# Threshold attention and a SwiGLU block on one core: the first batch's softmax scalings go to GpSimd

## The chip, the cores and the metric

The kernel runs on one core of one Trainium2 chip. A core has a matrix engine (TensorE, "PE" in the profile, with its weight loads as "PEld"), a vector engine (VectorE, "DVE"), a scalar engine (ScalarE, "ACT"), a general engine (GpSimd, "POOL") and a queue engine (SyncE, "SP") that issues most transfers. Each engine executes its own list of instructions in the order in which the program wrote them, and waits in front of an instruction whose operands are not ready. Results of TensorE land in a small accumulation memory of eight banks (PSUM); everything else lives in the on-chip memory (SBUF) with 128 partitions.

The metric is the device time of one execution in microseconds (us). The kernel before took 1361.29 us, the median of three runs (1361.02 to 1361.42).

## The reference

The inputs are q, k and v of 8 batches, 8 heads, 576 positions and 64 values each, a threshold tau, and the three weight matrices of a feed-forward block (512 to 1536 twice, 1536 to 512). Everything is float32.

```python
scores = (q @ k.T) / sqrt(64)
scores = where(scores >= max(scores) - tau, scores, -1e9)
attn = exp(scores - max(scores));  attn = attn / (sum(attn) + 1e-9)
x = (attn @ v)   # (8, 8, 576, 64), laid out as 4608 tokens of 512 values
g = x @ w_gate
out = (g * sigmoid(g) * (x @ w_val)) @ w_out
```

The attention of a batch needs all keys at once; the feed-forward block needs all eight heads of a token.

## The kernel before

The work goes through in two forms. **The first batch** (batch 0) is written out by hand. Its eight heads are four pairs; a pair's 576 queries are cut into four tiles of 128 rows (t = 0 to 3) and a tile of 64 rows (t = 4), in which both heads share the partitions. First the two early tiles (t = 0 and 1) of all four pairs are done, while keys, queries, values and weights are still arriving; then the tiles t = 2, 3 and 4 of all four pairs. The weights arrive in a raw form of two 32-bit words per number and are rebuilt beside the attention: ACT splits a piece (L330, L331), POOL clamps it (L323), DVE shifts it (L350) and joins its sign (L356), POOL adds its lower word (L366). Which of these steps comes after which point of which tile is written in the table `STEPS`, and in the second part in the loop itself.

**The other seven batches** form 84 slots. A planner (`Plan`) keeps a clock per engine, and every job carries an estimated duration. It emits the jobs of DVE, ACT, POOL and SP in the order of the estimated starts; the order on PE is that of the program. The estimates therefore set only the order, not the time.

One tile of the first batch passes through `scores` in five steps, and the loop over the tiles puts the steps of neighbouring tiles between each other:

1. The score products (L463) go into two PSUM tiles, one for each head, each of two banks. There are just these two tiles, so a product has to wait until the mask of the tile before has read the same head's scores. Then DVE finds each row's maximum (L480).
2. ACT forms the threshold (L483) and the exponentials (L484).
3. DVE masks them and sums the rows (L487), and forms the reciprocal `ri` of the sum (L489, L490). For t >= 2, head 0 is then scaled by `ri` on ACT (L497) and head 1 on POOL (L495).
4. For t < 2 the probabilities stay unscaled. In the next tile's turn ACT writes two diagonal matrices, `ident` times `ri` (L503).
5. After the next tile's score products and after the products with v of the tile before (`attend_tile`, L564 and L566), `flip_steps` turns the probabilities on PE: for t >= 2 by a transpose against the identity (L531, L539), for t < 2 by an ordinary product with the diagonal matrix (L533, L537), which scales in passing. ACT copies the result out of PSUM (L540, L547).

In the second part of the first batch the loop also puts products of the first feed-forward unit between the tiles (`fill`, L580, with L595, L596 on ACT, L604 on DVE and L611 on POOL). In tile t = 3 the first half of the turn of tile t = 2 stands ahead of the exponentials.

In POOL's own list a step of `scores` stands ahead of the clamp and the addition that the loop emits after it, and behind those that the loop emitted before it. Other POOL scalings are those of the queries: L403 in the first batch, L1912 in the slots, and L1847, which scales some of head 1's probabilities in the slots (the tables `POOLED` and `FIRST_POOLED` say how many).

All POOL scalings have one operation, such as

```python
nc.gpsimd.tensor_scalar(out=ps[x], in0=ps[x], scalar1=ri[:, x:x + 1], scalar2=None, op0=ALU.mult)
```

while the clamp, also on POOL, has two operations with constants (`min`, then `max`).

Of the kernel before, what the change touches and what calls it, by code (L numbers as in the profile page):

```python
# [14 lines left out]
ALU = mybir.AluOpType  # L15
# [129 lines left out]
def kernel(  # L145
# [107 lines left out]
    dbufs = deque(room(2 * P).rearrange("p (h q) -> p h q", h=2) for _ in range(2))  # L253
# [130 lines left out]
    def load_qk(i):  # L384
# [17 lines left out]
        def scale(x):  # L402
            nc.gpsimd.tensor_scalar(out=x, in0=x, scalar1=scl, scalar2=None, op0=ALU.mult)  # L403
# [50 lines left out]
    def scores(seg, t):  # L454
        qT, kT = seg["qT"], seg["kT"]
        q0 = t * P - seg["q0"]
        if t < NT:
            pss = [ps_s.tile([P, 2, 512], F32, name="sc") for _ in range(2)]
            for h, hs in enumerate(heads):
                cut_ = D if turned(t) and h == 1 else 0  # L460
                for n, lo, to in [(0, 0, D), (0, D, SH), (1, 0, SH)] if cut_ else [(0, 0, SH), (1, 0, SH)]:
                    at_ = (n * SH + lo - cut_) % S
                    nc.tensor.matmul(pss[h][:, n, lo:to], qT[hs, q0:q0 + P], kT[hs, at_:at_ + to - lo],  # L463
                                     start=True, stop=True)
# [26 lines left out]
        units = [ident] * m  # L491
        if t >= TA:
            for x in range(m):
                if x % 2:
                    nc.gpsimd.tensor_scalar(out=ps[x], in0=ps[x], scalar1=ri[:, x:x + 1], scalar2=None, op0=ALU.mult)  # L495
# [8 lines left out]
        unflipped.append((seg, t, both, [(p.rearrange("p n s -> p (n s)"), unit) for p, unit in zip(ps, units)]))  # L504
# [9 lines left out]
    def flip_steps():  # L514
# [8 lines left out]
        for h, (p, unit) in enumerate(ps):  # L523
# [3 lines left out]
            for kt in range(KT):  # L527
                at_ = kt * P + (D if turned(t) and h == 1 else 0)
                ks, to = slice(at_, at_ + P), slice(kt * P, (kt + 1) * P)
                if unit is ident:  # L530
                    nc.tensor.transpose(tp[:, to], p[:, ks], unit)  # L531
                else:
                    nc.tensor.matmul(tp[:, to], p[:, ks], unit, start=True, stop=True)  # L533
            if t < NT:
                if h == 1 and not turned(t):
                    for hs, (p_, unit_) in zip(heads, ps):
# [1598 lines left out]
```

## Time and profile before

| What | us |
|---|---|
| Median of three runs | 1361.29 |
| Profiled execution: first to last instruction (its own time is listed only as this span) | 1360.6 |
| PE busy | 1345.4 |
| DVE busy | 1067.0 |
| ACT busy | 880.6 |
| POOL busy | 714.9 |
| First tile's score products start (L463) | 7.83 |
| First score products of the second part of the first batch (t = 2) | 47.92 |
| First slot's score products start (L1776) | 128.88 |
| Granted clock of TensorE | 1.000 |

A line of a group in the profile reads: line of the kernel, engine, operation, output tile from input tiles, shapes, count, then busy time in us and the mean of one in ns, then the idle time of the engine just before and what ended it. A line of the timeline reads: start, length, engine, line, operation, tiles, shape, count, and in brackets the idle time before it and what ended that. A float32 product appears as two records, since TensorE goes over it twice; a transpose against the identity appears as one. The length of a merged line runs to the modelled end of its last record, so lines of one engine overlap a little; how long a group occupies PE is the distance to the start of the next group. A line of the waits reads: who waited for whom, the sum in us, the number of times and the longest.

### The profile page before, as it was taken

Reading aid. Unit: us, or ns where it says so; the run is one execution under the profiler, and the core shown is the slowest. Engines: PE = TensorE matmul, PEld = TensorE weight load, DVE = VectorE, ACT = ScalarE, POOL = GpSimd, SP = SyncE. Lnnn points to the kernel's source line nnn. Section 1 sums busy time; section 2 is a strip of 40 time slices with the busy share of each in tenths; the row PEclk is TensorE's granted clock in tenths of the full one; section 3 lists DMA queues with packets and bytes.
Section 4 is the critical chain, followed back from the end, with each engine's and each line's share of the span. In section 5 each row is a group of like instructions: output and inputs, shape, how many; then the busy total and the mean of one; then the engine's idle time right before and its main releaser. Section 6 shows DMA issues by size and latency. Waiting matters only on the chain.

```text
span 1360.6 us, 39192 instructions
## 1 busy us (share of the span) xinstructions
PE 1345.4 (99%) x15590; PEld 1112.3 (82%) x15590; DVE 1067.0 (78%) x2815; ACT 880.6 (65%) x2280; POOL 714.9 (53%) x662
## 2 busy tenths in 40 slices
PE   9999999999999999999999999999999999999998
PEld 7777777787788788877887788877887788999998
DVE  7788898878887777787778877877778776787786
ACT  6888777777756767676766776776767674330330
POOL 3788497654565679434963387427943592000000
PEclk9999999999999999999999999999999999999999
DMA  8753323555425531654154514553155404424411
GB/s 184 200 181 98 77 60 110 163 157 144 138 52 160 147 93 36 194 145 114 37 172 129 156 30 131 140 148 87 52 178 145 114 27 141 159 78 147 158 60 32
DMA packets 208294, 162.32 MB, mean 119 GB/s; under 512 B 166128, under 2 KB 180464, under 8 KB 202736
## 3 DMA queue, kind: packets, MB, share of 16 engines
q1 hardware_dynamic: 204192, 158.90, 41.5%
q8 instruction: 124, 2.03, 0.6%
q10 hardware_dynamic: 3920, 0.92, 0.3%
q14 instruction: 58, 0.48, 0.1%
HBM read 138.28 MB, written 21.50 MB: 117 GB/s over the span
## 4 chain that ended last, share of the span: by engine, by line
PE 92%; DVE 3%; DMA 2%; POOL 1%; ACT 1%; issue 1%; SPq 1%; ACTq 0%; DVEq 0%; POOLq 0%
PE pb L1047 18%; PE pa L1047 12%; PE px L1529 12%; PE sc L1776 10%; PE xa L1873 9%; PE pe L1047 9%; PE po L1326 5%; PE py L1538 5%; PE pv L1251 2%; PE pg L1251 2%; PE sc L1208 2%; PE pe L1208 1%; PE sc L463 1%; PE sc L1529 1%; POOL pall L495 1%
## 5 line engine op out<-in xcount | busy, mean ns | idle before, releaser
L1824 DVE SCALAR_TENSOR_TENSOR pall<-sc,th,pall 128x288 f32<-128x288 f32 x504 | 243.8, 513 | 60.5 <-ACT pall L1822 43.8
L1047 PE MATMUL pb<-xall,big 128*128 128x256 f32 x1152 | 273.3, 380 | 0.0
L1822 ACT ACTIVATE pall<-sc,nm 128x288 f32<-128x288 f32 x504 | 232.0, 496 | 38.8 <-DVE pall L1824 38.7
L1047 PEld LDWEIGHTS pb<-xall,big 128*128 128x128 f32 x1152 | 216.5, 190 | 30.7 <-issue 2.5
L1852 DVE STREAM_TRANSPOSE pall<-pall 128x576 f32<-128x576 f32 x252 | 188.0, 762 | 32.0 <-ACT pall L1850 18.4
L1850 ACT ACTIVATE pall<-pall,ri 128x288 f32<-128x288 f32 x418 | 191.7, 527 | 24.5 <-DVE ri L1838 23.8
L1047 PE MATMUL pa<-xall,big 128*128 128x256 f32 x768 | 183.6, 382 | 0.0
L900 POOL TENSOR_TENSOR hall<-hall,tmp 128x512 f32<-128x512 f32 x80 | 102.3, 1279 | 138.7 <-DVE hall L1100 122.1
L1797 DVE TENSOR_REDUCE mx<-sc 128x2 f32<-128x576 f32 x168 | 125.3, 746 | 52.4 <-PE sc L1776 51.9
L1047 PEld LDWEIGHTS pa<-xall,big 128*128 128x128 f32 x768 | 142.9, 190 | 22.4 <-issue 4.3
L1776 PE MATMUL sc<-kT,qT 64*32 64x288 f32 (+1 forms) x5376 | 146.1, 345 | 2.6 <-issue 2.1
L1776 PEld LDWEIGHTS sc<-kT,qT 64*32 64x32 f32 x5376 | 94.9, 106 | 56.7 <-issue 21.4
L1047 PE MATMUL pe<-xall,big 128*128 128x256 f32 x576 | 137.2, 381 | 0.6 <-issue 0.6
L1873 PE MATMUL xa<-pall,vall 64*32 64x288 f32 x4032 | 128.9, 404 | 0.0
L1847 POOL TENSOR_SCALAR pall<-pall,ri 128x288 f32<-128x288 f32 x86 | 85.2, 1003 | 81.1 <-DVE ri L1838 80.4
L1047 PEld LDWEIGHTS pe<-xall,big 128*128 128x128 f32 x576 | 108.5, 190 | 17.4 <-issue 3.0
L1873 PEld LDWEIGHTS xa<-pall,vall 64*32 64x32 f32 x4032 | 73.9, 107 | 47.2 <-issue 5.6
L1832 ACT COPY sums<-sums 32x6 f32<-32x6 f32 x336 | 66.6, 198 | 29.6 <-DVE pall L1824 24.5
L900 POOL TENSOR_TENSOR tmp<-tmp 128x512 f32<-128x512 f32 x36 | 45.9, 1276 | 59.3 <-ACT tmp L1122 59.3
L1099 ACT ACTIVATE vall<-tmp 128x512 f32<-128x512 f32 x96 | 60.0, 628 | 25.6 <-DVE tmp L1112 10.3
L1538 PE MATMUL py<-wo,hall 128*128 128x256 f32 x336 | 74.8, 379 | 0.0
L1799 DVE TENSOR_REDUCE mx<-sc 128x1 f32<-128x288 f32 x168 | 74.7, 445 | 0.0
(258 smaller groups left out, 2473.9 us busy)
## 6 DMA issues: line engine op xcount, KB each, us to landing
big<-sums_hbm SPq DMA_DIRECT2D x42, 1024.0 KB, 5.3
big<-sums_hbm SPq DMA_DIRECT2D x48, 768.0 KB, 4.7
vall<-in_v_dram SPq DMA_DIRECT2D x112, 144.0 KB, 3.1
out_dram<-big SPq DMA_DIRECT2D x32, 256.0 KB, 3.3
qT<-in_q_dram SPq DMA_DIRECT2D x112, 72.0 KB, 4.8
kT<-in_k_dram SPq DMA_DIRECT2D x112, 72.0 KB, 3.1
wo<-in_moe_w_gate_dram SPq DMA_DIRECT2D x16, 384.0 KB, 3.8
wo<-in_moe_w_val_dram SPq DMA_DIRECT2D x16, 384.0 KB, 4.4
```

Source lines behind the costliest of these rows:

```text
L900: return lambda: nc.gpsimd.tensor_tensor(out=out, in0=a, in1=b, op=op)
L1047: nc.tensor.matmul(ps[:, i], w[:, k_, i * P:(i + 1) * P], x[:, k_, :], start=first and i == k_ == 0, stop=True, skip_group_check=True)
L1529: nc.tensor.matmul(ps, a[:, f, :], ws[n][:, f, :], start=bank_ not in begun, stop=True, skip_group_check=True)
L1538: nc.tensor.matmul(ps(), a[:, f, i * P:(i + 1) * P], operands[o][:, f, :], start=first and f == 0, stop=True, skip_group_check=True)
L1776: nc.tensor.matmul(pss[h][(slice(g * G, (g + 1) * G), *part)], qT[hs, col:col + G], kT[hs, c * SH + keys[0]:c * SH + keys[1]], start=True, ...
L1797: rs.append(job("DVE", 0.72, lambda n=n, tile_=tile_: nc.vector.tensor_reduce(out=mx[:, n:n + 2, 0], in_=tile_[:, :, 0:SH], axis=AX.X, op= ...
L1822: ej = job("ACT", 0.42, lambda x=x, n=n: nc.scalar.activation(ps[x], scs[x], AF.Exp, bias=nm[:, n:n + 1]), ej, masks.get((h, u - 1)), rank=0)
L1824: masks[x] = job("DVE", 0.45, lambda x=x, n=n: nc.vector.scalar_tensor_tensor(out=ps[x], in0=scs[x], scalar=th[:, n:n + 1], in1=ps[x], op0 ...
L1847: scaled.append(job("POOL", 1.02, lambda x=x, n=n: nc.gpsimd.tensor_scalar(out=x, in0=x, scalar1=ri[:, n:n + 1], scalar2=None, op0=ALU.mul ...
L1850: scaled.append(job("ACT", 0.46, lambda x=x, n=n: nc.scalar.activation(x, x, AF.Copy, scale=ri[:, n:n + 1]), rj, rank=rank))
L1852: seg["turned"].append(job("DVE", 0.72, lambda both=both: nc.vector.transpose(out=both, in_=both), *scaled, rank=rank))
L1873: nc.tensor.matmul(holds[a].ap()[x * G:(x + 1) * G, 0:SH].rearrange("d (i q) -> d i q", q=G), vr[rs, h, j, ds], p[rs, h, :, j, :], start=( ...
```

## The change

Every scaling on POOL gets a second operation, a multiplication by the constant 1.0. In the first batch every probability is scaled on POOL right after `ri`: for t < 2 both heads, which were not scaled there before, and for t >= 2 both heads, of which ACT scaled head 0 before. For t = 4 the one tile moves from ACT to POOL. The diagonal matrices are gone, with their buffers, and all full 128-column turns are transposes against the identity; the products that turn the last 64 keys (L537) stay ordinary products, now with the identity. The score products of a tile come in the order head 0, head 1, head 0, head 1, where they came head 0, head 0, head 1, head 1; in the tiles t = 2 and 3, where head 1's first half is cut in two, head 1 has three products and the order is 0, 1, 1, 0, 1. In the planner two estimates change: a pooled scaling from 1.02 to 0.4 us and the scaling of a slot's queries from 1.75 to 0.7 us.

```diff
-    dbufs = deque(room(2 * P).rearrange("p (h q) -> p h q", h=2) for _ in range(2))
...
-            nc.gpsimd.tensor_scalar(out=x, in0=x, scalar1=scl, scalar2=None, op0=ALU.mult)
+            nc.gpsimd.tensor_scalar(out=x, in0=x, scalar1=scl, scalar2=1.0, op0=ALU.mult, op1=ALU.mult)
...
-            for h, hs in enumerate(heads):
-                cut_ = D if turned(t) and h == 1 else 0
-                for n, lo, to in [(0, 0, D), (0, D, SH), (1, 0, SH)] if cut_ else [(0, 0, SH), (1, 0, SH)]:
-                    at_ = (n * SH + lo - cut_) % S
-                    nc.tensor.matmul(pss[h][:, n, lo:to], qT[hs, q0:q0 + P], kT[hs, at_:at_ + to - lo],
-                                     start=True, stop=True)
+            cut_ = D if turned(t) else 0
+            second = [(1, 0, 0, D), (1, 0, D, SH), (1, 1, 0, SH)] if cut_ else [(1, 0, 0, SH), (1, 1, 0, SH)]
+            firsts = [(0, 0, 0, SH), (0, 1, 0, SH)]
+            order = [firsts[0], *second[:-1], firsts[1], second[-1]]
+            for h, n, lo, to in order:
+                hs = heads[h]
+                at_ = (n * SH + lo - h * cut_) % S
+                nc.tensor.matmul(pss[h][:, n, lo:to], qT[hs, q0:q0 + P], kT[hs, at_:at_ + to - lo],
+                                 start=True, stop=True)
...
-        units = [ident] * m
-        if t >= TA:
-            for x in range(m):
-                if x % 2:
-                    nc.gpsimd.tensor_scalar(out=ps[x], in0=ps[x], scalar1=ri[:, x:x + 1], scalar2=None, op0=ALU.mult)
-                else:
-                    nc.scalar.activation(ps[x], ps[x], AF.Copy, scale=ri[:, x:x + 1])
+        for x in range(m):
+            nc.gpsimd.tensor_scalar(out=ps[x], in0=ps[x], scalar1=ri[:, x:x + 1], scalar2=1.0, op0=ALU.mult, op1=ALU.mult)
         yield
-        if t < TA:
-            units = [dbufs[0][:, x, :] for x in range(m)]
-            dbufs.rotate(1)
-            for x in range(m):
-                nc.scalar.activation(units[x], ident, AF.Copy, scale=ri[:, x:x + 1])
...
-                if unit is ident:
-                    nc.tensor.transpose(tp[:, to], p[:, ks], unit)
-                else:
-                    nc.tensor.matmul(tp[:, to], p[:, ks], unit, start=True, stop=True)
+                nc.tensor.transpose(tp[:, to], p[:, ks], ident)
...
-                    scaled.append(job("POOL", 1.02, lambda x=x, n=n: nc.gpsimd.tensor_scalar(
-                        out=x, in0=x, scalar1=ri[:, n:n + 1], scalar2=None, op0=ALU.mult), rj, rank=1))
+                    scaled.append(job("POOL", 0.4, lambda x=x, n=n: nc.gpsimd.tensor_scalar(
+                        out=x, in0=x, scalar1=ri[:, n:n + 1], scalar2=1.0, op0=ALU.mult, op1=ALU.mult), rj, rank=1))
...
-        sj = job("POOL", 1.75, lambda: nc.gpsimd.tensor_scalar(out=box["t"][0], in0=box["t"][0], scalar1=scl, scalar2=None, op0=ALU.mult),
+        sj = job("POOL", 0.7, lambda: nc.gpsimd.tensor_scalar(out=box["t"][0], in0=box["t"][0], scalar1=scl, scalar2=1.0, op0=ALU.mult,
+                                                                       op1=ALU.mult),
```

More of the change, by code (lines that the diff above doesn't have):

```diff
@@ L490, in scores @@
         nc.vector.reciprocal(out=ri[:, 0:m], in_=tot[:, 0:m])
-        units = [ident] * m
-        if t >= TA:
-            for x in range(m):
-                if x % 2:
-                    nc.gpsimd.tensor_scalar(out=ps[x], in0=ps[x], scalar1=ri[:, x:x + 1], scalar2=None, op0=ALU.mult)
-                else:
-                    nc.scalar.activation(ps[x], ps[x], AF.Copy, scale=ri[:, x:x + 1])
-        yield
-        if t < TA:
-            units = [dbufs[0][:, x, :] for x in range(m)]
-            dbufs.rotate(1)
-            for x in range(m):
-                nc.scalar.activation(units[x], ident, AF.Copy, scale=ri[:, x:x + 1])
-        unflipped.append((seg, t, both, [(p.rearrange("p n s -> p (n s)"), unit) for p, unit in zip(ps, units)]))
+        for x in range(m):
+            nc.gpsimd.tensor_scalar(out=ps[x], in0=ps[x], scalar1=ri[:, x:x + 1], scalar2=1.0, op0=ALU.mult, op1=ALU.mult)
+        yield
+        unflipped.append((seg, t, both, [p.rearrange("p n s -> p (n s)") for p in ps]))
         yield
@@ L522, in flip_steps @@
         end = None
-        for h, (p, unit) in enumerate(ps):
+        for h, p in enumerate(ps):
             tp = bank("tp")
@@ L529, in flip_steps @@
                 ks, to = slice(at_, at_ + P), slice(kt * P, (kt + 1) * P)
-                if unit is ident:
-                    nc.tensor.transpose(tp[:, to], p[:, ks], unit)
-                else:
-                    nc.tensor.matmul(tp[:, to], p[:, ks], unit, start=True, stop=True)
+                nc.tensor.transpose(tp[:, to], p[:, ks], ident)
             if t < NT:
                 if h == 1 and not turned(t):
-                    for hs, (p_, unit_) in zip(heads, ps):
-                        nc.tensor.matmul(end[hs, 0:P], p_[:, KM:S], unit_, start=True, stop=True)
+                    for hs, p_ in zip(heads, ps):
+                        nc.tensor.matmul(end[hs, 0:P], p_[:, KM:S], ident, start=True, stop=True)
                 elif h == 1:
-                    nc.tensor.transpose(end[:, 0:P], both, unit)
+                    nc.tensor.transpose(end[:, 0:P], both, ident)
                 nc.scalar.copy(pT[:, h], tp.rearrange("p (t q) -> p t q", q=P))
@@ L542, in flip_steps @@
                 for hs in heads:
-                    nc.tensor.matmul(end[hs, 0:D], p[hs, KM:S], unit[hs, hs], start=True, stop=True)
+                    nc.tensor.matmul(end[hs, 0:D], p[hs, KM:S], ident[hs, hs], start=True, stop=True)
                 nc.scalar.copy(pT, tp.rearrange("p (t h q) -> p h t q", h=2, q=D))
```

## The prediction, made before the result was known

> **What bounds the kernel now.** First the split of the time by stage, from the busy time of the engines in five windows (length of the window, then busy us and instructions of PE, PEld, DVE, ACT and POOL, then clock, DMA share, GB/s). Three of them carry it:
>
> ```profile
> 16.50:48.50 32.00, 31.75 (x278) 25.55 (x279) 29.26 (x64) 31.45 (x73) 17.40 (x14) 1.00 0.82 193
> ...
> 55.00:131.00 76.00, 71.63 (x586) 54.88 (x584) 61.02 (x114) 66.19 (x127) 66.73 (x44) 1.00 0.48 148
> ...
> 146.00:1360.60 1214.60, 1208.14 (x14470) 1005.58 (x14468) 949.35 (x2563) 760.35 (x2027) 615.00 (x588) 1.00 0.40 114
> ```
>
> The reader sees that the slots (from 146 us on) have a PE that is busy for 1208.1 of 1214.6 us. There the change alters no PE work, so it can only move the moment at which PE gets there: everything is decided in the first 146 us. In the early tiles (16.5 to 48.5) PE, ACT and DVE are all near full, so it has to be asked which of them the others wait for. The waits of DVE in 16 to 49, then those of PE after 160:
>
> ```profile
> DVE nm L480 <- PE sc L463: 1.2, 4, 0.5
> DVE pall L487 <- ACT pall L484: 0.9, 2, 0.4
> ```
>
> ```profile
> PE sc L1776 <- issue: 2.1, 3, 1.1
> PE pe L1047 <- issue: 0.6, 1, 0.6
> ```
>
> In the early tiles DVE, which the change doesn't relieve, waits for only 2.1 us: whatever PE and ACT gain there, no more than about that comes through. In the slots PE waits for no engine at all. Third, the second part of the first batch, by PE's timeline around the tile t = 3 of one pair, and POOL's beside it:
>
> ```profile
> 79.57 1.04 PE L531 MATMUL tp<-pall 128*128 128x128 f32 x8
> 80.45 0.27 PE L539 MATMUL end<-pall 128*128 128x128 f32 x1
> ...
> 84.96 0.49 PE L566 MATMUL xa<-big,vends 128*128 128x128 f32 x2
> 85.58 0.66 PE L531 MATMUL tp<-pall 128*128 128x128 f32 x4
> 86.74 0.66 PE L531 MATMUL tp<-pall 128*128 128x128 f32 x4 [0.50 <-POOL pall L495]
> 87.23 0.27 PE L539 MATMUL end<-pall 128*128 128x128 f32 x1
> ```
>
> ```profile
> 77.86 1.87 POOL L495 TENSOR_SCALAR pall<-pall,ri 128x576 f32<-128x576 f32 x1 [0.38 <-DVE ri L490]
> 79.70 1.41 POOL L323 TENSOR_SCALAR big<-big 128x768 f32<-128x768 f32 x1
> 81.07 1.81 POOL L366 TENSOR_TENSOR big<-big,extra 128x768 uint32<-128x768 uint32 x1
> 82.85 1.83 POOL L366 TENSOR_TENSOR big<-big 128x768 uint32<-128x768 uint32 x1
> 84.67 2.02 POOL L495 TENSOR_SCALAR pall<-pall,ri 128x576 f32<-128x576 f32 x1
> 86.66 0.82 POOL L323 TENSOR_SCALAR big<-big 128x768 f32<-128x768 f32 x1
> ```
>
> A turn of eight transposes that waits for nothing holds PE 0.88 us (79.57 to 80.45). The turn of t = 3 starts 0.30 late (L566 holds 0.62 to the next group, 0.32 elsewhere) and takes 1.65, because head 1's scaling began only when POOL's two additions were done. These waits are what the change can take away. The products and L604 (DVE) behind that turn move with it: DVE waits for PE at L604 for 2.8 us in three places there.
>
> **The change part by part.** *The price of a scaling.* One-operation rows: 1003 ns for 288 columns (L1847), 1724 for 576 (L1912), so 0.28 us and 2.5 ns a column. The only two-operation row on POOL is the clamp, median 827 ns for 768 columns. By proportion 576 columns cost 0.62; with 0.28 fixed, 0.28 + 576 x 0.71 ns = 0.69. I take 0.66 (and 0.45 for 288). But the clamp's scalars are constants and the new scaling reads `ri`, one value for each partition. No row has both. The upper bound is L495's 1.87, the lower 0.62. I take the clamp's side: the gap between the rows is in the price of each column, and a value that is fetched once for each partition should add to the fixed part.
>
> *Early tiles, PE.* The turn of t < 2 holds PE 1.88 us (L533 at 29.88 to L537 at 31.76) and becomes 0.88: 8 tiles x 1.0 = 8.0 us of PE. It reaches the end only where DVE waits for a late PE: at 23.25 (0.51) and 44.42 (0.20). The other two waits (0.26 each, at 17.75 and 38.92) follow the release of a bank and stay. Gain 0.7.
>
> *Early tiles, ACT.* Sixteen diagonals go, 16 x 0.437 = 7.0 us by their lengths. One of them stands right ahead of a late exponential, at 39.75, and DVE then waits 0.45 at 41.33. Gain 0.4. Together 1.1, between 0 and the 2.1 of the waits.
>
> *Early tiles, POOL.* Sixteen scalings are added, 16 x 0.66 = 10.6 us on a POOL that is busy 17.4 of 32. PE turns a tile about 2.2 us after its `ri` (32.88 to 35.11), two scalings take 1.4 with the semaphore, so they lie beside the next scores. They cost in two other ways. (a) They run beside L350 and L356 on DVE, which follow `ri` directly at 27.56 and 32.79. How POOL and DVE disturb each other: L356 took 1.27 instead of 0.95 when the clamp ran (126.30), 0.95 inside an L495 (64.92), L350 1.15 instead of 0.54 when a clamp ran (70.28). I take 0.32 at two places, 0.6 in all; between 0 and both scalings in full, 2 x 1.3. (b) In tile 1 the new scalings stand ahead of the clamp (17.60), for which L350 (19.16) waits on DVE: POOL 17.8 to 19.2, clamp to 20.0, so L350 0.8 late, of which DVE's next wait and PE's lateness at 21.97 take a part. Loss 0.3, between 0 and 0.8.
>
> *Order of the heads.* Where both banks are free the heads overlap already: eight records of 0.24 hold PE for 1.18 (21.97 to 23.15), not 1.94. Where head 1's bank comes 0.82 later (one L487), head 1's first product now stands ahead of head 0's second, and head 0's maximum, for which DVE waits at 17.75 and 38.92, comes some 0.3 later. The end of the group stays. Loss 0.5, between 1.0 lost (three places) and 1.0 won (eight cut groups from 1.30 to 1.18).
>
> Early tiles together: 1.1 - 0.6 - 0.3 - 0.5 = 0.3 lost.
>
> *Second part, turns of t = 3.* What the four turns lose now, against 0.32 for L566 and 0.88 for the turn: 0.31 + 0.61 (65.09, 65.72), 0.30 + 0.77 (84.96, 85.58), 0.29 + 0.77 (104.61, 105.23) and 0.63 (125.00), together 3.7. Head 0 leaves ACT, where it stood behind L330 and L331; on POOL both heads stand behind the additions, which end at 84.67 (a little earlier, since the pair before took 1.3 in place of 1.87). Head 0 is ready at about 85.3, head 1 at 86.0, where PE wants them at 85.28 and 85.72. That leaves 0.1 to 0.3 at a turn. Gain 3.2, between 1.5 (the additions late by as much as a scaling in each) and 3.7. For t = 4 the one scaling joins POOL's list behind an addition that ends at 89.27; its turn is at 92.24, so it is hidden.
>
> *The rest.* ACT loses twelve L497 of 0.80; DVE waits there 7.4 us for exponentials, but these follow a turn's copy (L540) in ACT's list, so I count 0, with up to 1.5 for a gate product (L611) that leaves L356's way earlier. The faster query scalings (L403) are hidden behind loads. In the slots, POOL's faster scalings and the planner's other order cost and bring nothing, since PE waits for none of them; the 0.5 before the second slot's scores is the only wait near, so between 1.0 lost and 1.0 won. SP gets no new instruction, and its loads wait for the same places.
>
> The sum, on the profiled execution: 1360.6 - 3.2 + 0.3 = 1357.7 of span. The profile gives no time around the span; the median of the runs is 0.7 above it, so 1358.4.
>
> **The rivals.** *A, the scaling isn't faster.* If the pointer to `ri` or the form costs what L495 costs, 28 scalings are added or moved onto POOL at 1.9 us: 16 in the early tiles are 30 us on a POOL that has 15 idle there and some 4 between the first `ri` and 16.5; 12 in the second part are 23 us against 9 idle. About 11 + 14 = 25 us slower, since what ACT and PE win doesn't help a POOL that is last: 1386. For it speaks that no row shows the form; against it that the one-operation rows are dear by the column. It decides from about 1.0 us a scaling on, where 28 of them fill those idle 28 us. *B, POOL and DVE block each other for whole scalings.* L350 held up until the clamp's end at 70.28 speaks for it, the L356 inside L495 against it. Then the two places cost 1.3 each, tile 1 its 0.8 and the order its 1.0: 4.7 lost, 1.1 won, 3.2 won later, so 0.4 slower: 1361.7. [...] *C, DVE is not as full as it looks.* If the blocked L350 and L356 (1.4 and 2.0 at the worst, some 7 us over their medians in the first batch) come out of POOL's way, the freed PE time gets through: some 3 us more in the second part and 2 early, 1353.
>
> **How the numbers follow.** The forecast, with all its terms near their values: 0.54. C: 0.13. B: 0.23. A: 0.10. About 0.2% (2.7 us) is what a measurement of this kernel can tell from no change. The forecast's own range, 1355.5 to 1361, lies two thirds beyond that line and one third within: faster 0.36 + 0.13 = 0.49; same 0.18 + 0.14 of B = 0.32; slower 0.10 + 0.09 of B = 0.19. The range leaves out A and the ends of B and C: at the top 1.0 + 2.6 + 0.8 lost early and 1.5 won later give 2.9 slower, 1364; at the bottom C's 1353.
>
> **What would show it.** Right: POOL's L495 for 576 columns at 0.6 to 0.7 us, with 36 of them; tp of the early tiles with eight records each, 0.88 to the next group; the turns of t = 3 without a wait for POOL; the first slot's scores (now 128.88) at about 126. Wrong: L495 near 1.9 and PE waiting for it in every early tile (A); the second part's first scores (now 47.92) later than 49, with L350 and L356 long beside L495 (B); or earlier than 46.5 (C). The slots from there on should have the same length to within 1 us; if not, the planner's order has done more than I gave it.

## The result, and the profile after

The change made the kernel slower. Its median is 1368.51 us (1366.39 to 1369.29, four runs) beside 1361.15 (1360.96 to 1361.42) for the kernel before on the same chip: a ratio of 1.0048, with a 95% interval of 1.0036 to 1.0059. A later set of runs of the unchanged new kernel gave 1366.07 (1362.67 to 1369.86, eight runs) beside 1361.16, ratio 1.0038 (1.0025 to 1.0052). The forecast was 1358.4, with a range that ended at 1364.

The windows of the three stages after the change (length, then busy us and instructions of PE, PEld, DVE, ACT and POOL, clock, DMA share, GB/s):

```profile
16.50:48.50 32.00, 27.50 (x214) 19.36 (x212) 27.62 (x61) 27.24 (x57) 21.68 (x23) 0.89 0.79 192
55.00:131.00 76.00, 69.48 (x507) 53.10 (x501) 60.28 (x109) 55.43 (x112) 64.50 (x53) 0.96 0.48 145
146.00:1360.60 1214.60, 1212.72 (x14560) 1010.97 (x14559) 954.62 (x2576) 767.10 (x2047) 550.87 (x592) 1.00 0.40 114
```

In the early tiles PE, DVE and ACT are all less busy than before, and POOL, which is busier, has 10 of 32 us to spare; in the second part all four are less busy. In the early tiles no engine is near full any more; they wait for one another. New is the column before the last two: the granted clock is 0.89 and 0.96, where it was 1.00. The waits of DVE in 16.5 to 48.5 and those of PE from 160 us on, which answer to the two shown of before:

```profile
DVE nm L482 <- PE sc L465: 3.6, 4, 1.5
DVE pall L489 <- ACT pall L486: 0.3, 1, 0.3
```

```profile
PE sc L1765 <- issue: 0.9, 2, 0.5
```

DVE's waits for the exponentials shrank as foreseen (0.9 to 0.3); those for PE, which was to become faster, grew from 1.2 to 3.6. PE in turn waits for DVE's masks in front of its scores; its longest such wait in the early tiles, after and then before:

```profile
41.55 1.95 PE L465 MATMUL sc<-pall,qT 64*128 64x288 f32 x8 [1.43 <-DVE pall L489]
```

```profile
37.68 1.94 PE L463 MATMUL sc<-pall,qT 64*128 64x288 f32 x8 [0.25 <-DVE pall L487]
```

The slots are as full as before. So the loss lies where the forecast had put its gain. In the profiled execution (span 1367.4) the scores of t = 2 start at 52.59 where they started at 47.92 (4.7 later), and the first slot at 137.08 where it was 128.88 (8.2 later); from there to the end the kernel after is 1.4 shorter, which is no more than these stretches differ by between the traces of this document (1229 to 1232).

**The clock.** Cut along the places where it changes, with the window ahead of each:

```profile
4.26:7.67 3.41, 1.35 (x6) 0.85 (x5) 1.42 (x4) 1.09 (x1) 0.00 (x0) 1.00 0.93 135
7.67:11.08 3.41, 3.16 (x10) 2.01 (x11) 1.39 (x6) 0.44 (x3) 0.48 (x1) 0.50 0.90 243
14.50:17.91 3.41, 2.09 (x15) 1.06 (x14) 3.26 (x7) 2.47 (x6) 1.08 (x2) 1.00 1.04 144
17.91:21.32 3.41, 3.38 (x12) 2.26 (x14) 2.03 (x6) 2.37 (x6) 2.22 (x3) 0.50 0.65 169
21.32:24.74 3.42, 3.42 (x25) 3.09 (x22) 3.35 (x9) 1.99 (x5) 0.55 (x2) 0.50 1.02 257
...
79.35:82.77 3.42, 1.72 (x7) 0.86 (x5) 3.38 (x8) 2.63 (x6) 2.35 (x1) 1.00 0.37 81
82.77:86.18 3.41, 3.39 (x25) 2.53 (x24) 2.33 (x6) 1.01 (x1) 2.96 (x5) 0.50 0.95 376
86.18:89.59 3.41, 3.41 (x18) 3.13 (x15) 2.41 (x2) 1.88 (x6) 2.52 (x2) 0.50 0.18 18
```

Three times a stretch of 3.41 us in which PE was busy for only 1.35 to 2.09 is followed by one or two such stretches at a clock of 0.50. The second begins 3 windows of 3.41 us behind the first and the third 19 behind the second, so all lie on one grid. In none of the stretches ahead was PE idle throughout, only less busy. That this is what halves the clock is my reading of these three places; experiment 9 puts it to the test.

**The wait in front of 82.09.** PE waits 1.71 us there for a mask of DVE (0.83 before). PE, DVE's list, then POOL's, of the kernel after:

```profile
82.09 3.21 PE L465 MATMUL sc<-pall 64*128 64x288 f32 x10 [1.71 <-DVE pall L489]
```

```profile
74.82 1.05 DVE L349 TENSOR_SCALAR big<-big 128x768 uint32<-128x768 uint32 x1
76.58 1.18 DVE L349 TENSOR_SCALAR big<-big 128x768 uint32<-128x768 uint32 x1 [0.71 <-POOL big L322]
...
79.41 1.80 DVE L355 SCALAR_TENSOR_TENSOR big<-wo,big 128x768 uint32<-128x768 uint32 x2
81.13 0.81 DVE L489 SCALAR_TENSOR_TENSOR pall<-sc,th,pall 128x576 f32<-128x576 f32 x1
```

```profile
72.79 1.83 POOL L365 TENSOR_TENSOR big<-big 128x768 uint32<-128x768 uint32 x1
74.71 0.74 POOL L494 TENSOR_SCALAR pall<-pall,ri 128x576 f32<-128x576 f32 x1
75.54 1.80 POOL L322 TENSOR_SCALAR big<-big 128x768 f32<-128x768 f32 x2
```

The scaling of t = 4 (L494, 0.74 us) now stands in POOL's list ahead of a clamp (L322). DVE's second shift (L349) waits for that clamp, and the maxima, the joins (L355) and the mask (L489), for which PE waits, are queued behind the shift. Before, the clamp stood right behind the addition, and the two shifts ran in a row without a wait; PE, DVE and POOL there:

```profile
76.70 2.06 PE L463 MATMUL sc<-pall 64*128 64x288 f32 x10 [0.83 <-DVE pall L487]
```

```profile
70.28 1.62 DVE L350 TENSOR_SCALAR big<-big 128x768 uint32<-128x768 uint32 x2
```

```profile
68.39 1.82 POOL L366 TENSOR_TENSOR big<-big 128x768 uint32<-128x768 uint32 x1
70.20 0.82 POOL L323 TENSOR_SCALAR big<-big 128x768 f32<-128x768 f32 x1
```

### The profile page after: what moved, and what is told of

Same layout as the page of the kernel before. It is cut to its first block, busy times and chain, and to the rows that moved or that the text cites. A ratio compares the mean times of both kernels' runs of the same rounds, so it can differ in the third digit from the quotient of the medians.

```text
span 1367.4 us, 39127 instructions
## 1 busy us (share of the span) xinstructions
PE 1344.5 (98%) x15526; PEld 1109.1 (81%) x15526; DVE 1073.2 (78%) x2815; ACT 869.1 (64%) x2252; POOL 657.6 (48%) x690
## 4 chain that ended last, share of the span: by engine, by line
PE 91%; DVE 3%; DMA 2%; POOL 1%; issue 1%; SPq 1%; ACT 1%; ACTq 0%; DVEq 0%; POOLq 0%
PE pb L1036 18%; PE pa L1036 12%; PE px L1518 12%; PE sc L1765 10%; PE xa L1862 9%; PE pe L1036 9%; PE po L1315 5%; PE py L1527 5%; PE pv L1240 2%; PE pg L1240 2%; PE sc L1197 2%; PE pe L1197 1%; PE sc L465 1%; PE sc L1518 1%; DVE nm L482 1%
## 5 line engine op out<-in xcount | busy, mean ns | idle before, releaser
L1836 POOL TENSOR_SCALAR pall<-pall,ri 128x288 f32<-128x288 f32 x86 | 42.5, 506 | 92.7 <-DVE ri L1827 92.1
```

## The experiments

The theories were: the clock theory (PE has become too idle, its clock is halved, and that costs the most), the contention theory (POOL's scalings beside DVE's work, and the queue behind them) and the order theory (the two heads in turns). All times below are medians, each beside the kernel before on the same chip. Stage lengths and clocks by place come from one profiled execution of each kernel, which need not be a typical one.

**1. The early turns as ordinary products again.**

```diff
-                nc.tensor.transpose(tp[:, to], p[:, ks], ident)
+                if t < TA:
+                    nc.tensor.matmul(tp[:, to], p[:, ks], ident, start=True, stop=True)
+                else:
+                    nc.tensor.transpose(tp[:, to], p[:, ks], ident)
```

> The changed kernel with one thing put back: the eight turns of each early tile (t below 2) are ordinary products with the identity again (two passes each), while GpSimd still scales both heads there. That adds some 1 us of TensorE work in each of 8 tiles. Clock theory (the plain transposes leave TensorE too idle in the early tiles, so that its clock is halved there, and this costs most of the 6.8 us): the granted clock is 1.00 between 16 and 48 us, the three half-clock stretches shrink or go, and the kernel comes out at 1360 to 1364 although it does more work. Contention theory (what costs is GpSimd's scalings beside VectorE's joins and the queue behind them): these stay as they are, so 1367 to 1370, or up to 1376 if the added work is all exposed. Order theory (the two heads in turns let the first maximum start late): no change, 1367 to 1370.

Measured: 1364.85 beside 1361.12, ratio 1.0026 (1.0016 to 1.0036). More work for PE and less time, as the clock theory said, though the time lies above the range that it gave (1360 to 1364). The clock was 1.00 in the early tiles, which took 32.7 us (16.8 to 49.5) where the kernel after needs 34.7; the half clock near 82 stayed and another came at 121.7.

**2. The early tiles as before** (diagonals on ACT, nothing scaled on POOL), all else as changed.

```diff
-        for x in range(m):
-            nc.gpsimd.tensor_scalar(out=ps[x], in0=ps[x], scalar1=ri[:, x:x + 1], scalar2=1.0, op0=ALU.mult, op1=ALU.mult)
+        if t >= TA:
+            for x in range(m):
+                nc.gpsimd.tensor_scalar(out=ps[x], in0=ps[x], scalar1=ri[:, x:x + 1], scalar2=1.0, op0=ALU.mult, op1=ALU.mult)
...
+        if t < TA:
+            units = [dbufs[0][:, x, :] for x in range(m)]
+            dbufs.rotate(1)
+            for x in range(m):
+                nc.scalar.activation(units[x], ident, AF.Copy, scale=ri[:, x:x + 1])
```

> The changed kernel with the early tiles as they were before: ScalarE scales the diagonals, ordinary products turn with them, GpSimd scales nothing there. The scalings by two operations, GpSimd for both heads from t = 2 on and the new order of the score products stay. Clock theory: as with the ordinary products alone, granted clock 1.00 up to 48 us, 1360 to 1363. Contention theory: the early loss goes as well, and what is left is the gain of the second part, 1357.5 to 1359.5. Order theory: the loss stays, 1364 or more. What this kernel differs by from the one with ordinary products and GpSimd's scalings is the price of those scalings in the early tiles.

Measured: 1364.95, ratio 1.0029 (1.0017 to 1.0040). A miss for all the theories' numbers but the order theory's, which experiment 4 rules out: the early tiles were as short as before (31.4 us, 16.73 to 48.16), and 3.8 us of loss were still there. They lie behind the early tiles, which no theory had said: the second part took 84.2 us (81.0 before), with a half clock from 78.6 to 85.4.

**3. The form alone**, in the kernel before: every POOL scaling with two operations, and the planner's two costs.

```diff
-nc.gpsimd.tensor_scalar(out=ps[x], in0=ps[x], scalar1=ri[:, x:x + 1], scalar2=None, op0=ALU.mult)
+nc.gpsimd.tensor_scalar(out=ps[x], in0=ps[x], scalar1=ri[:, x:x + 1], scalar2=1.0, op0=ALU.mult, op1=ALU.mult)
```

> The kernel before with nothing changed but GpSimd's scalings, which have two operations in place of one wherever they are, with the planner's costs for them. Who scales what, the turns and the order of the products are those of before. Prediction's step on the second part: it takes 0.4 to 0.7 off the wait of the turns of t = 3 in each of four pairs, so 1358 to 1360.5, if the scaling of the second head decides there; ScalarE's scaling of the first head would keep some of it. Clock theory: no early transposes, so no half clock, granted clock 1.00. If GpSimd and VectorE block each other more with the quick form, 1361.5 or more.

Measured: 1362.27, ratio 1.0009 (1.0000 to 1.0017), with a whole clock in the batch. The scaling itself was faster, and the gain of the second part didn't come (80.8 us, 81.0 before).

**4. The old order of the heads** in the kernel after.

```diff
-            order = [firsts[0], *second[:-1], firsts[1], second[-1]]
+            order = [*firsts, *second]
```

(The edit put the old loop back, which gives this order.)

> The changed kernel with the score products in the order of before (all of the first head, then all of the second). Order theory: 4 us or more are won back, 1362 to 1364.5. My prediction put the order at a loss of 0.5, so 1367 to 1369 by it and by the contention theory. Clock theory: the half-clock stretches stay, give or take one window of 3.4 us, so 1365 to 1370.

Measured: 1366.30, ratio 1.0036 (1.0022 to 1.0049). The order theory falls; its half-clock stretches were elsewhere (39.5 to 46.4 and 80.5 to 87.3).

**5. The second part alone, with and without t = 4.** In the kernel before, with the quick form, POOL scales everything from t = 2 on (`e8`), or both heads of t = 2 and 3 while ACT keeps the one unit of t = 4 (`e7`). The planner's two estimates stay those of before. The edit of `e7`, against the kernel before with the quick form, stands below; in `e8` the line on GpSimd stands for every unit.

```diff
-                if x % 2:
+                if m == 2:
                     nc.gpsimd.tensor_scalar(out=ps[x], in0=ps[x], scalar1=ri[:, x:x + 1], scalar2=1.0, op0=ALU.mult, op1=ALU.mult)
                 else:
                     nc.scalar.activation(ps[x], ps[x], AF.Copy, scale=ri[:, x:x + 1])
```

> The kernel before with the scalings by two operations, and with GpSimd scaling every unit from t = 2 on (both heads of t = 2 and 3, and the one of t = 4). Early tiles, turns, order of products and the planner's costs are those of before. My prediction's gain of the second part alone: 3.2 off, so 1358. Theory from the trace after (the scaling of t = 4 stands ahead of the clamp in GpSimd's queue, VectorE's shift waits for the clamp, the mask of that tile ends later and TensorE waits 1.7 us in place of 0.83 in front of the next tile of t = 2; that idle stretch then halves the clock for 6.8 us): 3 x 0.86 slower for the wait and some 3 for the clock, less 1 to 2 for the turns of t = 3, so 1362.5 to 1366, with a half-clock stretch near 78 to 86 us.

> The same, but the one unit of t = 4 is scaled by ScalarE as before; GpSimd scales both heads of t = 2 and 3. Theory from the trace after: the wait in front of t = 2 of the next pair is 0.83 us again (in the second pair of the second part), no half-clock stretch, and the gain of the turns of t = 3 is left, so 1358.5 to 1360.5. If the half clock does not come from that wait, it is there in this kernel too, 1362 or more. If the turns of t = 3 gain nothing whoever scales, 1360.5 to 1361.5.

Measured: 1365.74 with t = 4 on POOL, ratio 1.0025 (1.0015 to 1.0036), and 1361.51 with t = 4 on ACT, ratio 0.9997 (0.9988 to 1.0006). One scaling of 0.74 us in each pair, moved off the engine that had time for it, costs 4.2 us. Of the executions with it on POOL, the two at a mean granted clock of 1.000 took 1363.38 and 1363.60, the six at 0.996 or 0.997 took 1363.91 to 1367.17. PE around the place with t = 4 on POOL, then with it on ACT:

```profile
77.51 2.45 PE L463 MATMUL sc<-pall 64*128 64x288 f32 x10 [1.70 <-DVE pall L487]
79.89 1.12 PE L561 MATMUL xa<-big,vall 128*64 128x64 f32 x16
```

```profile
77.59 2.06 PE L463 MATMUL sc<-pall 64*128 64x288 f32 x10 [0.38 <-DVE pall L487]
79.58 0.69 PE L564 MATMUL xa<-big,vall 128*64 128x64 f32 x16
```

The wait is 1.70 against 0.38, and the products behind it (`xa`, 16 records) take 1.12 at half clock, 0.69 at the whole one. But with t = 4 on ACT there was no gain either: the 1 to 3 us that were expected of the turns of t = 3 are missing. Such a turn, and POOL beside it, in that kernel:

```profile
85.92 0.49 PE L566 MATMUL xa<-big,vends 128*128 128x128 f32 x2
86.66 0.66 PE L531 MATMUL tp<-pall 128*128 128x128 f32 x4 [0.25 <-POOL pall L495]
88.19 0.66 PE L531 MATMUL tp<-pall 128*128 128x128 f32 x4 [0.88 <-POOL pall L495]
```

```profile
83.75 1.82 POOL L366 TENSOR_TENSOR big<-big 128x768 uint32<-128x768 uint32 x1
85.67 2.47 POOL L495 TENSOR_SCALAR pall<-pall,ri 128x576 f32<-128x576 f32 x2
```

Both scalings stand behind POOL's additions, and the pair took 2.47 us, beside a shift, a maximum and a join of DVE; undisturbed it takes 1.47 (27.67 in the kernel after). PE waits for both heads. Against the same floors as in the prediction, the four turns lose 4.3 us here, 3.7 before.

**6. The form alone with the old planner costs.**

```diff
-                    scaled.append(job("POOL", 0.4, lambda x=x, n=n: nc.gpsimd.tensor_scalar(
+                    scaled.append(job("POOL", 1.02, lambda x=x, n=n: nc.gpsimd.tensor_scalar(
```

(and 1.75 again for the query scaling)

> The kernel before with the scalings by two operations and nothing else, the planner's costs too are those of before, so every engine's list is that of before. With the planner's new costs the same kernel took 1362.27 beside 1361.12 of the kernel before, and in its trace the first slot was 0.85 us longer, by a wait of TensorE for a mask on VectorE, of which the list was another one. If the new costs did that: 1360 to 1361.2 here, the first slot 10.4 us as before. If the quick form itself holds VectorE up in the slots: 1362 or more.

Measured: 1361.64 beside 1361.61, ratio 1.0000 (0.9991 to 1.0009). By itself the quick form is worth nothing that the runs can tell: its turns of t = 3 lose 3.2 in place of 3.7, and the scores behind them wait longer for a mask (1.05 in place of 0.89 at 116). The first slot was 11.1 long here too, so my reading that the new costs had lengthened it was a miss.

**7. The new order alone**, in the kernel before.

> The kernel before with the score products of the two heads in turns and nothing else. My prediction put the new order at a loss of 0.5: 1361.6 (1361 to 1362.5). In the kernel with the diagonals kept, the tile at 16.5 us and those after it started 0.2 us later than in the one with the old order, which would make 1361.3. Order theory (it costs some us): 1363 or more.

Measured: 1362.74 beside 1361.61, ratio 1.0006 (0.9996 to 1.0016). No verdict beyond "small"; 0.5 is inside. In its trace the early tiles took 31.3 us (31.4 before) and the second part 81.5 (81.0), so if the order costs 0.5, it does so behind the early tiles and not in them.

**8. Both causes put back in the kernel after, and one of them.** `e10` lets ACT scale the unit of t = 4; `e11` has the ordinary early turns of experiment 1 as well. The unchanged kernel (`a2`) ran beside them.

```diff
         for x in range(m):
-            nc.gpsimd.tensor_scalar(out=ps[x], in0=ps[x], scalar1=ri[:, x:x + 1], scalar2=1.0, op0=ALU.mult, op1=ALU.mult)
+            if m == 1:
+                nc.scalar.activation(ps[x], ps[x], AF.Copy, scale=ri[:, x:x + 1])
+            else:
+                nc.gpsimd.tensor_scalar(out=ps[x], in0=ps[x], scalar1=ri[:, x:x + 1], scalar2=1.0, op0=ALU.mult, op1=ALU.mult)
```

> The changed kernel with one thing put back: the one unit of t = 4 is scaled by ScalarE, as before. In the kernel with GpSimd for the later tiles only, this step took 4.2 (1365.74 to 1361.51). Theory of two causes (the idle stretch in front of t = 2 in the second part, and the idle stretches of the early tiles): the half-clock stretch near 82 us goes, the early ones stay, 1363.5 to 1365.5. If all comes from the early tiles: 1367.5 to 1369.

> The changed kernel with both put back: the early turns are ordinary products with the identity, and ScalarE scales the one unit of t = 4. GpSimd still scales both heads in the early tiles and in t = 2 and 3. Theory of two causes: the granted clock stays at 1.00 (but for the stretch of one window that can come at 7 to 11 us in any of these kernels), 1360.5 to 1363, although it does about 8 us more of TensorE work in the early tiles than the changed kernel. If something else in the early tiles costs (GpSimd beside VectorE): 1364 or more.

> The changed kernel once more, unchanged, for the spread of the half-clock stretches and a comparison on one chip with the kernels that put its parts back. Clock theory: 1366 to 1369.5, with the stretches where TensorE waits most (16 to 25, 36 to 46, 79 to 86 us), each a whole number of 3.41 us long, and not the same in every execution.

Measured on one chip, beside 1361.16: unchanged 1366.07; t = 4 on ACT 1363.51, ratio 1.0020 (1.0010 to 1.0031); the early turns as well 1361.58, ratio 1.0005 (0.9995 to 1.0015). Of a loss of 4.9 us, the first edit takes back 2.6 and the second 1.9; all the rest of the change is worth 0.4, which can't be told from nothing. Singly the two steps are near the edge of what the intervals can tell; together they are clear of it. The unchanged kernel's executions lie 7 us apart and follow the clock: 1369.5 and 1369.9 at a mean of 0.993, 1362.7 and 1364.8 at 0.997. The two stages in the unchanged kernel (its slowest execution, 1369.86), then with both put back:

```profile
18.00:52.80 34.80, 29.59 (x228) 20.61 (x229) 30.28 (x63) 30.10 (x64) 25.57 (x26) 0.90 0.77 196
52.80:137.20 84.40, 77.92 (x565) 59.08 (x566) 68.34 (x128) 61.43 (x124) 70.72 (x59) 0.96 0.45 139
```

```profile
18.00:50.70 32.70, 31.29 (x277) 24.30 (x277) 29.59 (x63) 29.55 (x63) 25.97 (x26) 1.00 0.85 207
50.70:131.50 80.80, 76.08 (x576) 57.47 (x577) 67.02 (x128) 63.94 (x127) 68.61 (x56) 1.00 0.48 145
```

The second part is back at the length of before (81.0). The early tiles are still 1.3 longer than before (31.4), at a whole clock. In the trace of `e10`, where the early tiles are those of the kernel after, they took 32.7 as well (16.76 to 49.44), with one window at half clock (40.7 to 44.1) in place of two.

**9. Useless work to hold the clock.** First in the kernel of 5 with everything from t = 2 on POOL: three idle products where PE waits for the late mask.

```diff
+            if n > NP and not x:
+                run_idle(3)
             go = scores(seg, t)
```

> The kernel in which GpSimd scales every unit from t = 2 on (1365.74), with three products more in front of the scores of t = 2 of the last three pairs: six records of 0.21 us with no use, in a wait of TensorE of 1.70 us. All else, the late mask too, is as in that kernel. Clock theory: the window that ends at 79 us has TensorE busy for 3.0 us in place of 1.7, the clock is not halved near 79 to 86 us, and the time is that of the runs without a loss of the clock, 1363.4 to 1364.2. If the mask's lateness alone makes the 4.2: 1365.5 to 1367, the added products bring nothing or cost.

Measured: 1363.32 beside 1361.16, ratio 1.0016 (1.0007 to 1.0025), where the kernel without them stood at 1.0025. DVE's second shift waits for the clamp as before (0.71), yet the clock is whole:

```profile
75.64:79.05 3.41, 1.71 (x10) 1.46 (x10) 3.34 (x10) 2.46 (x5) 2.51 (x2) 1.00 0.67 157
79.05:82.46 3.41, 3.41 (x26) 2.54 (x25) 2.76 (x3) 0.51 (x2) 3.33 (x4) 0.50 0.78 307
```

```profile
76.67:80.08 3.41, 3.01 (x16) 2.37 (x16) 3.34 (x9) 2.48 (x5) 2.46 (x1) 1.00 0.57 164
80.08:83.49 3.41, 3.41 (x35) 2.88 (x34) 2.49 (x4) 1.88 (x5) 3.10 (x4) 1.00 0.80 307
```

(first without, then with the idle products). Nor is this only so in the two traces: a mean granted clock of 0.997 or less came in 6 of 8 executions without the idle products and in 1 of 10 with them. This shows that it is PE's idle time that halves the clock there. It splits the loss of the second part too: 84.2 us with both, 83.3 with the late mask and a whole clock, 80.8 with neither. So the half clock is 0.9 of it in the traces and the late mask 2.5. By the medians, each against the kernel before on its chip (4.1 with both, 2.2 with the late mask, -0.1 with neither), they are 2.0 and 2.3.

Then the same in the kernel after: two idle products ahead of the early tiles' scores and three in the late places (`e13`), only the late ones (`e17`), only the early ones (`e18`); and, in the kernel with t = 4 on ACT, only the early ones (`e14`).

```diff
+            if 0 < n < NP or (n == NP and not x):
+                run_idle(2)
+            if n > NP and not x:
+                run_idle(3)
             go = scores(seg, t)
```

> The changed kernel with nothing taken back, only useless work added: two idle products (four records of 0.21 us, 0.85) in front of the scores of the early tiles of pairs 2 to 4 and of the first tile of the second part, where TensorE waited 1.3 us in the mean, and three (1.28) in front of the scores of t = 2 of its last three pairs, where it waited 1.7. Clock theory: the half-clock stretches near 18 and 82 us go, 1361 to 1363.5, 4 us or more under the changed kernel. If the clock is not the cause: 1366 to 1372, as all added work only costs.

> The changed kernel with only the late idle products (three in front of the scores of t = 2 of the last three pairs), no early ones. If they win what they won beside the early tiles of before (2.4): 1363.5 to 1365, no half clock near 82 us, the early ones stay. If they bring nothing beside the changed early tiles: 1366 to 1368, and then they are what made the kernel with both sets slow.

> The changed kernel with only the early idle products (two in front of the scores of the early tiles of pairs 2 to 4 and of the first tile of the second part). In the traces the early tiles took 34.8 us with a half clock, 33.1 with these products, 32.7 with a whole clock and no idle products: 1.7 shorter, so 1364 to 1366.5, with the half clock near 82 us as before. If the early set is what costs: 1367 to 1369.

> The changed kernel with ScalarE for the unit of t = 4 (1363.51, of which the runs with a granted clock of 0.995 took 1367 and those with 0.999 took 1362) and the two idle products in front of the scores of the early tiles. Clock theory: no half clock but the one window at 7 to 11 us in part of the executions, 1360 to 1361.8, and if the rest of the change gains what the runs by clock point to, under the kernel before. If the plain turns and GpSimd's scalings cost by themselves in the early tiles: 1362 or more.

Measured: both sets 1366.48 beside 1361.29, ratio 1.0036 (1.0023 to 1.0048); late only 1367.29 beside 1362.26, 1.0035 (1.0022 to 1.0047); early only 1366.35, 1.0030 (1.0020 to 1.0041); early in the kernel with t = 4 on ACT 1363.10 beside 1361.29, 1.0013 (1.0005 to 1.0022). Against 1.0038 for the unchanged kernel these are no gains that the intervals can tell from none, so **the clock theory's number failed**. Its mechanism didn't: the mean granted clock was 0.999 or 1.000 in all five executions with both sets, and 0.997 or less in all twelve of the unchanged kernel. In the trace the clock was whole from 12 us on, and the stages became shorter by 1.7 and 1.3 (34.8 and 84.4 in the unchanged kernel):

```profile
18.00:51.20 33.20, 31.27 (x253) 21.85 (x253) 29.30 (x63) 28.91 (x63) 26.48 (x26) 1.00 0.83 204
51.20:134.30 83.10, 78.40 (x591) 59.98 (x594) 67.19 (x128) 62.01 (x124) 72.74 (x58) 1.00 0.47 141
```

Beside 31.4 and 81.0 before, 1.8 and 2.1 are left at a whole clock. That is what the waits and the idle products cost together, and no run separates the two. The idle products are not free: with them and a whole clock the early tiles took 33.1 in the traces of `e14` and `e18` too, more than the 32.7 of `e10` without them and with a window at half clock. And the traces compare unlike executions: that of the unchanged kernel is its slowest (1369.86, median 1366.07), that with both sets its median (1366.48). The idle products took away the executions with little clock (1365.31 to 1367.96 with them, 1362.67 to 1369.86 without) and left the median where it was.

**10. A longer start.** Eight idle products in place of six at the very start, in the kernel of `e14` (`e15`) and in the kernel before (`e16`).

> The same with eight idle products in place of six at the very start (16 records of 0.43 at half clock, 0.21 at full), so that TensorE's wait in front of the first scores at 7.8 us shrinks from 1.1 to 2.3 us to nothing or 1.5. Clock theory: the one window at 7 to 11 us, which costs 1.4, comes less often, so 0.2 to 0.8 under the kernel without it. If that stretch comes from something else: the same time within 0.3, or up to 0.8 more where the idle products end after 7.8 us.

> The kernel before with eight idle products in place of six at the very start and nothing else. Clock theory: the runs with a granted clock of 0.999 (1362 beside 1360.8 of those with 1.000) become fewer, so 0.2 to 0.6 faster in the median. If that stretch has another cause: no change, or up to 0.8 slower.

Measured: 1363.19, ratio 1.0007 (0.9998 to 1.0016), beside 1.0013 without; and 1362.16, ratio 1.0006 (0.9997 to 1.0015). No gain. In the kernel before, a mean clock under 1.000 came in 9 of 27 executions and then in 2 of 11, and those at 1.000 got slower (median 1361 to 1362); in the kernel of `e14` it came in 5 of 11 and then in 6 of 11. In the trace of `e15` the one window at half clock lies near 142 us, in the slots, and none at the start. So it isn't shown that the longer start keeps the window at 7 to 11 us away, nor that this window is what sets apart the executions under 1.000.

No kernel of these is measurably faster than the one before.

## Why the prediction was wrong, step by step

The profiled execution of the unchanged kernel in experiment 8 (span 1368.0, against 1360.6) reaches the first slot 8.3 us late. By the stages: 1.5 by the half clock at the start, 3.4 in the early tiles (forecast 0.3 lost), 3.4 in the second part (forecast 3.2 won). It is the slowest of that kernel's eight executions there; by the medians the kernel lost 4.9 in those runs and 7.4 in the first ones. The 0.7 that the prediction added to the span compares two executions: in every execution of the kernel before for which both are listed, its time is 2.1 to 2.2 above its span, so the profiled one took some 1362.7 (an estimate from these), 1.4 over the median. The sum isn't changed by this, but the spans here are compared with a longer than usual execution of before.

- **The price of a scaling: right in kind, a little small.** 0.74 us for 576 columns undisturbed (forecast 0.66), 506 ns for 288 (0.45), with the 36 scalings of 576 that were expected. Rival A falls. What was mis-sized is the price in company: the pair takes 2.31 to 2.47 beside DVE's L349 and L355. A pair of an early tile, record by record, then the join that ran beside it:

```profile
31.09 0.90 POOL L494 TENSOR_SCALAR pall<-pall,ri 128x576 f32<-128x576 f32 x1 [0.16 <-DVE ri L492]
31.96 1.44 POOL L494 TENSOR_SCALAR pall<-pall,ri 128x576 f32<-128x576 f32 x1
```

```profile
31.41 1.38 DVE L355 SCALAR_TENSOR_TENSOR big<-wo,big 128x768 uint32<-128x768 uint32 x1
```

  The join, 0.95 alone, began inside the first scaling and took 0.43 longer; the second scaling, 0.74 alone, began inside the join and took 0.70 longer. Where a join and a scaling began together, at 69.64, the join took 0.95 and the scaling 1.55. That is what one of the two waiting for the instruction of the other to end would give, to within 0.14 us. The prediction asked what POOL's scalings do to DVE; it never asked what DVE does to the scalings.
- **Early tiles, PE: the turn is as short as said, the gain of 0.7 isn't there.** 0.96 to the next group at whole clock (33.16 in the kernel after), but the time it freed became idle time in front of the next scores (1.43 where it was 0.25). **The step that failed is that this idle time was counted as free.** The prediction never asked what TensorE's granted clock does when PE idles, and no rival did. By these traces the half clock is 1.7 to 2.1 of the 3.4 lost here (34.8 against 33.2 and 32.7 at a whole clock, experiments 9 and 8); one has the idle products and the other the ordinary turns, and what the plain early tiles take at a whole clock was not measured.
- **Early tiles, POOL and the order: (a) and (b) of about the right size, the order not there.** (a) Two joins of 1.38 us where they took 0.96 and 1.11, so 0.69 in place of 0.6. (b) L349 waited 0.5 for a clamp behind the scalings in the kernel of experiment 1 and in that with t = 4 on ACT (forecast 0.3). The order was put at 0.5 in these tiles, and they were no longer by it (31.3 and 31.4 in the traces of experiments 7 and 2). With both causes put back the early tiles lose 1.3 at a whole clock, where (a) and (b) had been put at 0.9; whether anything of the 1.1 gain beside them came stays open, since that kernel has the ordinary turns.
- **Second part, turns of t = 3: gain 3.2, the largest term, and false.** They lost 0.6 instead (experiment 5). The working put both heads behind the additions on POOL and took 1.3 us for the pair; the pair took 2.47, so both heads came later than ScalarE and GpSimd had delivered them side by side. Where a turn did get faster (experiment 6, 0.5 in all), the next wait for a mask took part of it (1.05 where it was 0.89 at 116 us). That points to DVE's chain of shifts, joins and masks as what paces the second part; no run shortened that chain, so it is argued and not shown. The prediction had asked in the early tiles how much DVE waits for PE, and here took 2.8 us of such waits as room enough for a gain of 3.2.
- **The scaling of t = 4: "hidden", put at nothing, and it cost the most.** This is the second step that failed. The working looked at who needs the scaled unit (a turn, in good time) and not at who stands behind it on POOL (the clamp) and who waits for that (L349, and in DVE's list the mask). It cost 2.3 to 2.5 us as a late mask, and 0.9 to 2.0 as the half clock that the longer wait brings (experiment 9). The same question had been asked in step (b) for tile 1.
- **The rest: as said.** The planner's list and POOL's faster scalings in the slots bring nothing that the runs can tell; the slots came out 0.9 and 1.4 shorter in the two traces of the kernel after, which is inside their spread.
- **The rivals.** B came nearest: a slower kernel, with the sign that the prediction gave for it (the second part's first scores later than 49, joins long beside the scalings). The records of the new scaling fit a wait of the later of the two for the other's instruction to end, to within 0.14 us; those of the old form don't (before, at 64.05 and 64.92: 1.87 and 0.95, both as alone), and no run shows what makes the difference. What B had wrong is the price: it charged DVE with both scalings at each place, 1.3, where the join waited for the rest of one, 0.43 at the most; and it charged nothing to POOL, whose second scaling took up to 0.81 longer. C is out: DVE's work went off the path and time was lost.

## What to carry to other kernels

An instruction that is moved to another engine's list must be followed to the next one behind it in that list and to whoever waits for that one; a reader of the result that has time proves nothing. Time taken off an engine that is not the bound becomes idle time, and on TensorE idle time had a price of its own here (0.9 to 2.0 us in experiment 9): look at the granted clock behind windows of 3.41 us in which PE is less busy (1.34 to 2.09 us in those ahead of a half clock in the traces of the kernel after and of experiments 4 and 5). And two pieces of work that two engines did side by side need not be shortened by giving both to one faster engine, least of all when it is slowed by what runs beside it: 0.80 on ScalarE beside 1.87 on GpSimd became 2.47 for the pair.

## What the runs showed of the hardware that was not expected

- A second operation made POOL's scaling faster, not slower: 739 ns at the least for 576 columns (L494) against 1867 at the least for the one-operation form before (L495), though the second factor is 1.0. The slow form didn't disturb DVE's join nor the join it (before, at 64.05 and 64.92: 1.87 and 0.95, both as alone); the quick form and the join did hold each other up (after, 0.95 for the join and 0.74 for the scaling alone; 1.38 and 1.44 at 31.41 and 31.96, 0.95 and 1.55 at 69.64).
- The half clock came in whole windows of 3.41 us, one or two at a time, and where and how often it fell differs between executions of the same kernel (from 17.91 and 82.77 us on in the first trace of the kernel after, from 18.31 and 83.16 on in that of experiment 8; mean clocks of 0.993 to 0.997 there). The window at 7 to 11 us came in 8 of the 20 traces, three of them of kernels whose start is that of before (in experiment 5, with t = 4 on ACT, at 8.15 to 11.56; the scores that start at 16.50 in the kernel before start at 18.10), and not in the profiled execution of before: so the 1.5 us at the start of the kernel after may be chance and no part of the change's loss.
- Busy time alone does not say when. A window with 1.99 us of PE work was followed by no half clock, one with 2.09 was, both in the kernel after:

```profile
38.39:41.81 3.42, 1.99 (x17) 1.61 (x16) 3.42 (x7) 2.76 (x8) 3.34 (x4) 1.00 0.86 212
41.81:45.22 3.41, 3.39 (x30) 2.25 (x29) 2.79 (x8) 3.32 (x8) 2.97 (x5) 1.00 0.89 194
```

  Half of the work in the first window was transposes (1.04 us). They feel the clock too: eight of them held PE for 0.88 us at whole clock (before, at 79.57) and 1.70 at half clock (after, at 86.77). Their share doesn't say when either: of the work ahead of a half clock they were 1.31 of 2.09 us (14.50 to 17.91) and none of 1.72 (79.35 to 82.77). No run here settles what does.
- Left open: what the changed early tiles take at a whole clock without useless work, how the loss with the idle products splits into their own cost and that of the waits, and why the slots vary by 1229 to 1232 us between kernels with the same products in them.
